# A reciprocal root taken on 128x4 row sums and sent through memory, instead of on a broadcast 128x512 tile

## The chip, the cores and the metric

One core of a Trainium2 chip. The metric is the device time of one execution in microseconds (us); lower is better. Engines in the profile: PE does the matrix products (PEld its weight loads), DVE is the vector engine, ACT the scalar engine, POOL is GpSimd, and SP only issues DMA transfers. A line number such as L277 is a line of the kernel's file; the change shifts the numbers, so the same statement has another number after it.

## The reference

A spectral filter along the sequence, then a gated feed-forward block on the normalized result. Cut to what matters:

```python
X = np.fft.rfft(x, axis=1)              # x: (8, 3008, 256)
y = np.fft.irfft(X * F, n=3008, axis=1) # F: complex filter, (1505, 256)
t = y.reshape(24064, 256)
rms = np.sqrt(np.mean(t * t, axis=-1, keepdims=True) + 1e-06)
xn = t / rms * rms_g
g = xn @ w_gate                         # 256 -> 1536
out = (g * sigmoid(g) * (xn @ w_val)) @ w_out
```

The change is about `1 / rms`: one number for each of the 24064 tokens.

## The kernel before

Both transforms are done as small matrix products with two trips through memory (z and g). Channels lie on the 128 partitions and tokens along the row. A batch has 6 groups (m = 0 to 5) of 512 tokens, the last of 448, and a group has 12 slots of the feed-forward loop, so a batch is 72 slots and the kernel 576. In a slot `gv` makes gate and value, `down` the output product of two slots earlier. Units of the next batch are put into the slots by a table, `plan`, in program order; every engine takes its instructions in that order.

A sum over channels is a sum over partitions. The kernel before takes it with a 128x128 matrix of ones, which leaves the same sum in all 128 partitions, and then raises that full tile to the power -0.5 on POOL:

```python
def q_unit(b, m):
    sq = st[b]["sq"].pop(m)
    w = ntok(m)                                            # 512, or 448 for m == 5
    ps = psM.tile([P, 512], FP32, tag="mx", name="psq")
    for dh in range(2):
        nc.tensor.matmul(ps[:, 0:w], ones, sq[:, dh, 0:w], start=(dh == 0), stop=(dh == 1))
    u = up.tile([P, 512], FP32, tag="u", name="u")
    nc.scalar.activation(out=u[:, 0:w], in_=ps[:, 0:w], func=AXT.Identity, scale=1.0 / D, bias=epsb)
    st[b]["u"][m] = u

def xn_unit(b, m):
    ...
    nc.gpsimd.tensor_tensor(out=rho[:, 0:w], in0=u[:, 0:w], in1=mhalf.to_broadcast([P, w]),
                            op=ALU.pow)                    # L277
    ...
    nc.gpsimd.tensor_tensor(out=xn[:, :, 0:w], in0=y[:, :, 0:w],
                            in1=rho[:, 0:w].unsqueeze(1).to_broadcast([P, 2, w]), op=ALU.mult)  # L280
```

The part of the plan that matters (batch b is prepared while batch b - 1 is multiplied; t = 72 (b - 1)):

```python
for i in range(12):
    at(t + i, a_unit, b, i)                       # first transform; needs x in SBUF
    if i % 3 == 2:
        at(t + i + 1, z_store, b, i // 3)         # SP: 4 stores to memory
for c in range(4):
    at(t + 13 + 2 * c if c < 3 else t + 30, t2_load, b, c)   # SP: loads them back, transposed
for i in range(16):
    s0 = t + 20 + (i * 36) // 16
    at(s0, b_unit, b, i)                          # psb, then two products on DVE
    at(s0 + 3, bi_unit, b, i)                     # psi, evicted by ACT
    ...                                           # g_store at s0 + 5
...                                               # t4_load at t + 60 + c
for m in range(6):
    s0 = t + 64 + 6 * m
    at(s0, n_unit, b, m, 0)                       # psn: y and its squares
    at(s0 + 1, n_unit, b, m, 1)
    at(s0 + 3, q_unit, b, m)
    at(s0 + 4, xn_unit, b, m)
```

Group m of batch b is first used in slot t + 72 + 12 m. Ahead of the slots a prologue prepares batch 0 and its first two groups.

## Time and profile before

| | before |
|---|---|
| median of the runs | 4263.72 us (3 runs, 4261.08 to 4263.81) |
| POOL busy | 4021 of 4261 us, 94% |
| of that, the power | 3851 us, 48 times 71.8 or 81.9 us |
| PE busy | 25% |
| PE's wait for xn | 2010 us |

The page of the kernel before: the busy time of each engine; the rows of POOL and the granted TensorE clock in 40 slices (a digit is tenths); the lines of the chain that ended last.

```profile
PE 1047.3 (25%) x5952; PEld 596.1 (14%) x5952; DVE 589.5 (14%) x903; ACT 628.2 (15%) x1094; POOL 4021.3 (94%) x210
...
POOL 3999989999899998999989999899998999989997
PEclk9995666556655575556655666556655656666566
...
POOL rho L277 90%; POOL xn L280 2%; PE pg L295 1%; PE pv L295 1%; POOL xc L177 0%; DMA xc<-in_x_dram 0%; DMA t_252<-z_tmp 0%; PE psi L220 0%; DMA z_tmp<-t_237 0%; PE psa L185 0%; DMA z_tmp<-t_209 0%; ACT u L269 0%; PE psq L267 0%; PE psb L2
```

POOL is full from the third slice to the end, and the chain that ended last is the power for nine tenths of the span. PE's clock row reads 5 and 6: PE works in bursts and idles between them at half clock.

The groups of instructions by shape (count, then busy us and mean ns, then the idle time ahead of them and what ended it):

```profile
L277 POOL TENSOR_TENSOR rho<-u,mhalf 128x512 f32<-128x512 f32 x40 | 3277.0, 81924 | 186.5 <-ACT u L269 146.8 <-PE po_7988 L312 6.4 <-PE po_9510 L312 6.4
L277 POOL TENSOR_TENSOR rho<-u,mhalf 128x448 f32<-128x448 f32 x8 | 574.1, 71765 | 0.2
...
L280 POOL TENSOR_TENSOR xn<-y,rho 128x1024 f16<-128x1024 f32 x40 | 93.7, 2342 | 3.1
```

Two shapes of the same power give a slope: (81.92 - 71.77) / 64 = 0.159 us per column. A multiplication of twice as many elements on the same engine, L280, takes 2.34 us. So the power is dear per column, and the tile has 128 identical rows. The table of waits (us in total, times, longest) says who pays:

```profile
PE pg L295 <- POOL xn L280: 2010.4, 32, 81.8
```

What would bound the kernel if POOL did not is seen in the bursts. The timeline, plain slots near the end (start, duration; each is the first matmul of a slot):

```profile
4094.94 0.59 PE L295 MATMUL pg<-xn,wg 128*128 128x512 f16 x2
...
4096.24 0.59 PE L295 MATMUL pg<-xn,wg 128*128 128x512 f16 x2
```

A slot takes 1.30 us when PE has nothing to wait for. The table of windows shows the clock over one burst:

```profile
core 0: us, PE busy (x) PEld busy (x) DVE busy (x) ACT busy (x) POOL busy (x), PEclk, DMA share, GB/s
...
2005.00:2010.00 5.00, 5.00 (x19) 2.40 (x18) 2.38 (x4) 1.55 (x3) 4.92 (x2) 0.53 0.86 209
2010.00:2015.00 5.00, 5.00 (x36) 3.31 (x35) 3.34 (x6) 2.63 (x5) 5.00 (x1) 1.00 0.21 53
```

PE is busy for both stretches; in the first its mean granted clock is 0.53, in the second 1.00, and it gets through 36 matmuls instead of 19.

### The profile page before, as it was taken

The numbers are of one execution on the slowest core, as the hardware profiler recorded it, in microseconds if no ns is written. First come the engines' busy times: TensorE is split into PE (matmuls) and PEld (weight loads), VectorE is DVE, ScalarE is ACT, GpSimd is POOL, SyncE is SP. The second block draws the span as 40 slices with busy tenths as digits, with TensorE's granted clock in tenths as the row PEclk, the third lists the DMA queues.
The fourth block names the chain that finished last, engine by engine and source line by source line (L and its number), as shares of the span: only waits on it lengthen the run. The fifth ranks groups of instructions, "written<-read, shape, count | busy, mean of one in ns | idle before, by whom it ended". The sixth has DMA issues, their size and how long they took to land.

```text
span 4261.0 us, 16476 instructions
## 1 busy us (share of the span) xinstructions
PE 1047.3 (25%) x5952; PEld 596.1 (14%) x5952; DVE 589.5 (14%) x903; ACT 628.2 (15%) x1094; POOL 4021.3 (94%) x210
## 2 busy tenths in 40 slices
PE   3031232114221141212312232122311313221023
PEld 1021121002110030101201121011211202111011
DVE  3011110003100130002200121001210102110011
ACT  3021121002110021101111111111101201111011
POOL 3999989999899998999989999899998999989997
PEclk9995666556655575556655666556655656666566
DMA  7020010001100010000100001000110101000000
GB/s 153 0 46 12 16 39 23 12 0 39 29 23 12 10 42 16 23 13 15 38 16 23 13 23 29 16 23 12 25 27 16 36 0 25 25 8 5 0 10 15
DMA packets 82114, 96.78 MB, mean 23 GB/s; under 512 B 9672, under 2 KB 62408, under 8 KB 81744
## 3 DMA queue, kind: packets, MB, share of 16 engines
q1 hardware_dynamic: 71920, 77.95, 7.4%
q0 software_dynamic: 10112, 17.77, 2.5%
q8 instruction: 47, 0.77, 0.1%
q14 instruction: 35, 0.29, 0.0%
HBM read 60.56 MB, written 49.81 MB: 26 GB/s over the span
## 4 chain that ended last, share of the span: by engine, by line
POOL 93%; PE 4%; DMA 1%; issue 1%; ACT 0%; DVE 0%; SPq 0%; POOLq 0%; DVEq 0%; ACTq 0%
POOL rho L277 90%; POOL xn L280 2%; PE pg L295 1%; PE pv L295 1%; POOL xc L177 0%; DMA xc<-in_x_dram 0%; DMA t_252<-z_tmp 0%; PE psi L220 0%; DMA z_tmp<-t_237 0%; PE psa L185 0%; DMA z_tmp<-t_209 0%; ACT u L269 0%; PE psq L267 0%; PE psb L206 0%; PE po_12225 L312 0%
## 5 line engine op out<-in xcount | busy, mean ns | idle before, releaser
L277 POOL TENSOR_TENSOR rho<-u,mhalf 128x512 f32<-128x512 f32 (+1 forms) x48 | 3851.1, 80231 | 186.7 <-ACT u L269 146.8
L295 PE MATMUL pg<-xn,wg 128*128 128x512 f16 (+1 forms) x1152 | 376.8, 412 | 2476.9 <-POOL xn L280 2010.4
L300 DVE TENSOR_TENSOR hh<-pv,sg 128x512 f16<-128x512 f32 (+1 forms) x576 | 390.6, 679 | 3611.9 <-PE pv L295 2217.5
L299 ACT ACTIVATE sg<-pg 128x512 f16<-128x512 f32 (+1 forms) x576 | 339.1, 590 | 2274.7 <-PE pg L295 2272.6
L295 PEld LDWEIGHTS <-wg 128*128 128x128 f16 x1152 | 111.9, 103 | 2512.1 <-issue 2485.7
L295 PE MATMUL pv<-xn,wv 128*128 128x512 f16 (+1 forms) x1152 | 372.2, 407 | 0.0
L312 PEld LDWEIGHTS <-hh 128*128 128x128 f16 (+1 forms) x2304 | 236.7, 104 | 217.3 <-issue 130.6
L269 ACT ACTIVATE u<-psq,epsb 128x512 f32<-128x512 f32 (+1 forms) x48 | 32.6, 678 | 1134.4 <-POOL rho L277 1120.3
L295 PEld LDWEIGHTS <-wv 128*128 128x128 f16 x1152 | 121.6, 106 | 158.4 <-issue 48.0
L280 POOL TENSOR_TENSOR xn<-y,rho 128x1024 f16<-128x1024 f32 (+1 forms) x48 | 110.3, 2297 | 3.8
L206 PEld LDWEIGHTS <-wb 96*128 96x128 f16 x256 | 26.2, 107 | 491.7 <-issue 469.1
L220 PEld LDWEIGHTS <-wi 128*128 128x128 f16 x512 | 52.9, 106 | 112.9 <-issue 71.2
L258 ACT ACTIVATE y<-psn,gsb 128x512 f32<-128x512 f32 (+1 forms) x96 | 65.6, 683 | 19.7 <-PE psn L251 15.2
L185 PE MATMUL psa<-xc,wa 128*128 128x512 f16 x96 | 40.5, 428 | 107.1 <-DMA xc<-in_x_dram 97.8
L260 ACT ACTIVATE sq<-psn 128x512 f16<-128x512 f32 (+1 forms) x96 | 56.5, 589 | 0.0
L177 POOL DMA_DIRECT2D xc<-in_x_dram x64 | 34.8, 558 | 0.8 <-POOLq L474 0.8
L267 PE MATMUL psq<-sq,ones 128*128 128x512 f16 (+1 forms) x96 | 30.2, 394 | 2.3 <-ACT sq L260 2.3
L185 PEld LDWEIGHTS <-wa 128*128 128x128 f16 x96 | 9.8, 103 | 119.1 <-issue 101.0
L312 PE MATMUL po_11699<-wo,hh 128*128 128x256 f16 x24 | 5.3, 307 | 75.1 <-ACT o_11682 L317 75.1
L206 PE MATMUL psb<-t_2390,wb 96*128 96x256 f16 x8 | 2.0, 338 | 72.7 <-ACT u L269 72.7
L206 PE MATMUL psb<-t_3912,wb 96*128 96x256 f16 x8 | 2.0, 337 | 72.7 <-ACT u L269 72.7
L206 PE MATMUL psb<-t_5434,wb 96*128 96x256 f16 x8 | 2.0, 338 | 72.6 <-ACT u L269 72.6
(948 smaller groups left out, 1187.0 us busy)
## 6 DMA issues: line engine op xcount, KB each, us to landing
xc<-in_x_dram POOLq DMA_DIRECT2D x56, 192.0 KB, 4.7
wi<-wi_t SPq DMA_DIRECT2D x4, 512.0 KB, 12.2
xc<-in_x_dram POOLq DMA_DIRECT2D x8, 160.0 KB, 5.4
wb<-wb_t SPq DMA_DIRECT2D x1, 768.0 KB, 5.9
wg<-in_moe_w_gate_dram POOLq DMA_DIRECT2D x4, 192.0 KB, 13.1
wv<-in_moe_w_val_dram POOLq DMA_DIRECT2D x4, 192.0 KB, 12.4
wo<-in_moe_w_out_dram POOLq DMA_DIRECT2D x4, 192.0 KB, 13.2
out_dram<-o_874 SPq DMA_DIRECT2D x2, 256.0 KB, 3.8
```

The lines of the kernel that those rows point to most:

```text
L177: nc.gpsimd.dma_start(t[h * 64:h * 64 + 64, 0:w, :], rows[:, lo:lo + w, :])
L185: nc.tensor.matmul(ps, wa, st[b]["x"][c][:, 2 * r:2 * r + 2, :], start=True, stop=True)
L220: nc.tensor.matmul(ps[:, u, :], wi[:, 2 * i + u, q, :], s12[q][:, u, :], start=(q == 0), stop=(q == 1))
L258: nc.scalar.activation(out=y[:, dh, 0:w], in_=ps[:, 0:w], func=AXT.Identity, scale=gsb[:, dh:dh + 1])
L260: nc.scalar.activation(out=st[b]["sq"][m][:, dh, 0:w], in_=ps[:, 0:w], func=AXT.Square)
L269: nc.scalar.activation(out=u[:, 0:w], in_=ps[:, 0:w], func=AXT.Identity, scale=1.0 / D, bias=epsb)
L277: nc.gpsimd.tensor_tensor(out=rho[:, 0:w], in0=u[:, 0:w], in1=mhalf.to_broadcast([P, w]), op=ALU.pow)
L280: nc.gpsimd.tensor_tensor(out=xn[:, :, 0:w], in0=y[:, :, 0:w], in1=rho[:, 0:w].unsqueeze(1).to_broadcast([P, 2, w]), op=ALU.mult)
L295: nc.tensor.matmul(ps[:, 0:w], wt[:, dt_, ts(jt, P)], xn[:, dt_, 0:w], start=(dt_ == 0), stop=(dt_ == 1))
L299: nc.scalar.activation(out=sg[:, 0:w], in_=pg[:, 0:w], func=AXT.Silu)
L300: nc.vector.tensor_tensor(out=hh[:, 0:w], in0=pv[:, 0:w], in1=sg[:, 0:w], op=ALU.mult)
L312: nc.tensor.matmul(po[s4 // 2][0:w, s4 % 2, :], hh[:, s4 * P:s4 * P + w], wo[:, jt, :], start=(jt == 0 and s4 % 2 == 0), stop=(jt == JT - ...
```

## The change

Its intent: take the power once per token and not 128 times. The squares become the stationary operand and a single column of ones streams, so the sums of 512 tokens come out as a 128x4 tile with tokens on partitions. The power is taken there. To multiply y by it, the 512 numbers are needed along the row of every partition again: the 128x4 tile is stored to memory (16 contiguous bytes per partition) and loaded back with a broadcast to all 128 partitions. The trip takes time, so the plan computes the sums earlier and leaves slots between sums, trip and use. To make room the transform's units move to earlier slots too.

The diff, cut (pools, memory declaration, prologue, the plan of batch 0's later groups and the 448-token case left out):

```diff
     def q_unit(b, m):
         sq = st[b]["sq"].pop(m)
-        for dh in range(2):
-            nc.tensor.matmul(ps[:, 0:w], ones, sq[:, dh, 0:w], start=(dh == 0), stop=(dh == 1))
-        nc.scalar.activation(out=u[:, 0:w], in_=ps[:, 0:w], func=AXT.Identity, scale=1.0 / D, bias=epsb)
+        for q in range(4):
+            for dh in range(2):
+                nc.tensor.matmul(ps[0:w, q:q + 1], sq[:, dh, q * P:q * P + w], ones, ...)
+        nc.vector.tensor_scalar(out=u[0:w, a:e], in0=ps[0:w, a:e], scalar1=1.0 / D,
+                                scalar2=1e-6 * Y_SCALE * Y_SCALE, op0=ALU.mult, op1=ALU.add)
+        nc.gpsimd.tensor_tensor(out=rho, in0=u, in1=mhalf, op=ALU.pow)        # 128x4
+    def rho_move(b, m):
+        nc.sync.dma_start(r_d[b, m], st[b]["u"].pop(m))
+        nc.sync.dma_start(rb.rearrange("p a q -> p (a q)"),
+                          r_d[b, m].rearrange("p q -> (p q)").partition_broadcast(P))
     def xn_unit(b, m):
-        nc.gpsimd.tensor_tensor(out=rho[:, 0:w], in0=u[:, 0:w], in1=mhalf.to_broadcast([P, w]), op=ALU.pow)
-        nc.gpsimd.tensor_tensor(out=xn[:, :, 0:w], in0=y[:, :, 0:w], in1=rho[:, 0:w]..., op=ALU.mult)
+        rv = rb.rearrange("p t q -> p q t")                                   # stride of 16 bytes
+        nc.gpsimd.tensor_tensor(out=xv[:, :, 0:nq], in0=yv[:, :, 0:nq], in1=rv[:, 0:nq]..., op=ALU.mult)
...
+        def norm_plan(b, m, s0):
+            at(s0, n_unit, b, m, 0)
+            at(s0 + 1, n_unit, b, m, 1)
+            at(s0 + 3, q_unit, b, m)
+            at(s0 + 5, rho_move, b, m)
+            at(s0 + 10, xn_unit, b, m)
...
-                at(t + 13 + 2 * c if c < 3 else t + 30, t2_load, b, c)
+                at(t + 13 + c if c < 3 else t + 24, t2_load, b, c)
-                s0 = t + 20 + (i * 36) // 16
+                s0 = t + 16 + 2 * i
-                    at(s0 + 5, g_store, b, i // 2)
+                    at(s0 + 4, g_store, b, i // 2)
-                at(t + 60 + c, t4_load, b, c)
+                at(t + 53, t4_load, b, c)
-                s0 = t + 64 + 6 * m        (n, q and xn units at s0, +1, +3, +4)
+                norm_plan(b, m, t + 57 + 8 * m)
```

More of the change, by code (lines that the diff above doesn't have):

```diff
@@ L129 @@
     g_d = nc.dram_tensor("g_tmp", (B, K2, KR, D), FP16, kind="Internal").ap()
+    r_d = nc.dram_tensor("r_tmp", (B, 6, P, 4), FP32, kind="Internal").ap()
     glob = ctx.enter_context(tc.tile_pool(name="glob", bufs=1))
     xp = ctx.enter_context(tc.tile_pool(name="xp", bufs=4))
-    t1p = ctx.enter_context(tc.tile_pool(name="t1p", bufs=2))
+    t1p = ctx.enter_context(tc.tile_pool(name="t1p", bufs=3))
     t2p = ctx.enter_context(tc.tile_pool(name="t2p", bufs=3))
@@ L139 @@
     sqp = ctx.enter_context(tc.tile_pool(name="sqp", bufs=2))
-    rp = ctx.enter_context(tc.tile_pool(name="rp", bufs=1))
+    rp = ctx.enter_context(tc.tile_pool(name="rp", bufs=2))
     up = ctx.enter_context(tc.tile_pool(name="up", bufs=2))
@@ L159 @@
     gsb = glob.tile([P, 2], FP32)
-    ones = glob.tile([P, P], FP16)
-    mhalf = glob.tile([P, 1], FP32)
-    epsb = glob.tile([P, 1], FP32)
+    ones = glob.tile([P, 1], FP16)
+    mhalf = glob.tile([P, 4], FP32)
     st = {b: {"x": {}, "t1": {}, "t2": {}, "s": {}, "t3": {}, "t4": {}, "y": {}, "sq": {},
@@ L263, in q_unit @@
         sq = st[b]["sq"].pop(m)
-        w = ntok(m)
-        ps = psM.tile([P, 512], FP32, tag="mx", name="psq")
-        for dh in range(2):
-            nc.tensor.matmul(ps[:, 0:w], ones, sq[:, dh, 0:w], start=(dh == 0), stop=(dh == 1))
-        u = up.tile([P, 512], FP32, tag="u", name="u")
-        nc.scalar.activation(out=u[:, 0:w], in_=ps[:, 0:w], func=AXT.Identity, scale=1.0 / D, bias=epsb)
-        st[b]["u"][m] = u
+        ps = psM.tile([P, 4], FP32, tag="mx", name="psq")
+        for q in range(4):
+            w = P if 4 * m + q < H - 1 else 64
+            for dh in range(2):
+                nc.tensor.matmul(ps[0:w, q:q + 1], sq[:, dh, q * P:q * P + w], ones,
+                                 start=(dh == 0), stop=(dh == 1))
@@ new lines, in q_unit @@
+        u = up.tile([P, 4], FP32, tag="u", name="u")
+        rho = up.tile([P, 4], FP32, tag="rho", name="rho")
+        if m == 5:
+            nc.vector.memset(u, 1.0)
+            parts = ((P, 0, 3), (64, 3, 4))
+        else:
+            parts = ((P, 0, 4),)
+        for w, a, e in parts:
+            nc.vector.tensor_scalar(out=u[0:w, a:e], in0=ps[0:w, a:e], scalar1=1.0 / D,
+                                    scalar2=1e-6 * Y_SCALE * Y_SCALE, op0=ALU.mult, op1=ALU.add)
+        nc.gpsimd.tensor_tensor(out=rho, in0=u, in1=mhalf, op=ALU.pow)
@@ L272, in xn_unit @@
+        st[b]["u"][m] = rho
+    def rho_move(b, m):
+        nc.sync.dma_start(r_d[b, m], st[b]["u"].pop(m))
+        rb = rp.tile([P, P, 4], FP32, tag="rb", name="rb")
+        nc.sync.dma_start(rb.rearrange("p a q -> p (a q)"),
+                          r_d[b, m].rearrange("p q -> (p q)").partition_broadcast(P))
+        st[b]["u"][m] = rb
     def xn_unit(b, m):
-        w = ntok(m)
-        u = st[b]["u"].pop(m)
+        rb = st[b]["u"].pop(m)
         y = st[b]["y"].pop(m)
-        rho = rp.tile([P, 512], FP32, tag="rho", name="rho")
@@ L277, in xn_unit @@
-        nc.gpsimd.tensor_tensor(out=rho[:, 0:w], in0=u[:, 0:w], in1=mhalf.to_broadcast([P, w]),
-                                op=ALU.pow)
         xn = xnp.tile([P, 2, 512], FP16, tag="xn", name="xn")
-        nc.gpsimd.tensor_tensor(out=xn[:, :, 0:w], in0=y[:, :, 0:w],
-                                in1=rho[:, 0:w].unsqueeze(1).to_broadcast([P, 2, w]), op=ALU.mult)
+        nq = 4 if m < 5 else 3
+        yv = y.rearrange("p a (q t) -> p a q t", q=4)
+        xv = xn.rearrange("p a (q t) -> p a q t", q=4)
@@ new lines, in xn_unit @@
+        rv = rb.rearrange("p t q -> p q t")
+        nc.gpsimd.tensor_tensor(out=xv[:, :, 0:nq], in0=yv[:, :, 0:nq],
+                                in1=rv[:, 0:nq].unsqueeze(1).to_broadcast([P, 2, nq, P]),
+                                op=ALU.mult)
+        if nq < 4:
+            nc.gpsimd.tensor_tensor(out=xv[:, :, 3, 0:64], in0=yv[:, :, 3, 0:64],
+                                    in1=rv[:, 3, 0:64].unsqueeze(1).to_broadcast([P, 2, 64]),
+                                    op=ALU.mult)
@@ L366 @@
         nc.vector.memset(mhalf, -0.5)
-        nc.vector.memset(epsb, 1e-6 * Y_SCALE * Y_SCALE)
         for c in range(NC):
@@ L405 @@
             q_unit(0, m)
+            rho_move(0, m)
+        for m in range(2):
             xn_unit(0, m)
@@ L414, in at @@
             plan.setdefault(slot, []).append((fn, a))
-        for m in range(2, 6):
-            s0 = (m - 2) * 10
-            at(s0, n_unit, 0, m, 0)
-            at(s0 + 1, n_unit, 0, m, 1)
-            at(s0 + 3, q_unit, 0, m)
-            at(s0 + 4, xn_unit, 0, m)
+        def norm_plan(b, m, s0):
[4 more added lines that the diff above has]
+            at(s0 + 10, xn_unit, b, m)
+        for m in range(2, 6):
+            norm_plan(0, m, (m - 2) * 10)
         for b in range(1, B):
@@ L439 @@
             for c in range(4):
-                at(t + 60 + c, t4_load, b, c)
+                at(t + 53, t4_load, b, c)
             for m in range(6):
-                s0 = t + 64 + 6 * m
-                at(s0, n_unit, b, m, 0)
-                at(s0 + 1, n_unit, b, m, 1)
-                at(s0 + 3, q_unit, b, m)
-                at(s0 + 4, xn_unit, b, m)
+                norm_plan(b, m, t + 57 + 8 * m)
         stores = {}
```

## The prediction

> **What bounds the kernel now.** GpSimd. The page gives POOL 94% busy (4021 of 4261 us), PE 25%; the chain of waits is 90% the power (line 277). The groups by shape give it 81.92 us for 128x512 and 71.77 for 128x448, 48 times, 3851 us. A line through the two sizes is 0.65 us + 0.159 us per column; all 128 rows hold the same numbers (a ones matrix broadcasts the sum). PE waits 2010 us for xn.
>
> **What the change removes, adds, moves.**
> - The power shrinks to 128x4: 0.65 + 4 x 0.159 = 1.3 us (estimate), 62 us in all for 3851.
> - The xn multiplication (2.34 us for 1024 elements) stays on POOL, one operand now at a 16-byte stride. The Trainium skill, "GPSIMD Engine Reference", section 3.1, gives about 2.6 cycles per element for two inputs, near this trace's 2.1 ns; no run shows the stride's cost. I allow 2.3 to 5 us.
> - Row sums become 8 one-column matmuls with 8 weight loads instead of two 512-column ones: 0.45 to 0.85 us (loads of 0.105 us that partly overlap, as in the psn groups), against 0.43. The ACT eviction u (0.68 us) becomes a tiny DVE operation.
> - New: a 2 KB store and a 256 KB broadcast load per tile. Here a 96 KB store lands in 1.9 us, 96 KB loads in 2.2. I estimate 2 + 3 us, with SP blocked 2 us between. Row sums to xn is then about 10 us; a batch's first group has 12 slots (16 us), later ones more. Hidden, except in the prologue.
>
> **Then PE bounds it.** Bursts in the timeline show PE saturated at granted clock 1.00: 1.303 us per slot (gate, value, down), 1.417 in the 448-token groups. Added work: first transform 0.216 us, b and bi 0.65 per pair, psn 0.22.
> Per batch: 60 x 1.303 + 12 x 1.417 = 95; transform 2.6; b and bi 10.4; psn 2.6; row sums 3.9; small stalls 3 (ACT holding the two shared PSUM buffers: slots of 1.97 us instead of 1.74; about 1 us at the first b unit, because z-store to t2 landing takes 7 us and has about 6.5). That is 118. Seven, and a last of 100: 924.
> Prologue: the first power starts at 96.3 us today; power, store, load and xn put the first slot at about 105. Some 3 us for the cold clock (0.5 in the first 4 us of a burst; "TensorE: Matmul & The Clock Gate", part 1, says that sustained activity releases it, and this trace agrees). Tail 6. Sum 1037 us.
>
> **Predicted 1037 us, 1012 to 1085 holding it 8 times in 10.** Faster by over 2%: 0.985, within 2%: 0.01, slower: 0.005.
>
> **What would show it.** Power mean 1 to 2 us; POOL below 30% busy; PE near 95% busy, mean clock above 0.95; chain of waits led by PE lines 295 and 312; first slot at 103 to 108 us; plain slots of 1.30 us; xn not PE's main releaser after the first slot.
>
> **What would make it wrong.** A fixed cost of the small power, or a strided xn, far over these figures, so that xn arrives after its slot; SP blocked by the round trips, so that t2 or t4 loads come late, PE stalls several us a batch and its clock falls; row sums over 1 us a group; a clock that does not hold at 1.00 under steady load.

## The result

The median fell from 4262.4 us (4 runs, 4260.43 to 4263.81) to 1032.17 us (4 runs, 1031.0 to 1034.96). The ratio is 0.2423, with a 95% interval of 0.2417 to 0.2428. Ratios here are the mean time of one kernel's fast runs over that of the other's of the same rounds, so not quite the ratio of the medians quoted. The result is correct.

The page after, the lines that answer to those of before:

```profile
PE 931.7 (90%) x6240; PEld 565.0 (55%) x6240; DVE 591.7 (57%) x966; ACT 597.5 (58%) x1046; POOL 246.0 (24%) x218
...
PE   2162789999999999999999999999999999999997
...
POOL 5501423113410333013410333013410332023200
PEclk9999999999999999999999999999999999999999
...
PE pg L319 21%; PE pv L319 20%; PE psi L221 6%; PE psb L207 3%; ACT sq L261 2%; PE psn L252 1%; PE psa L186 1%; DMA fi_120<-in_filt_i_dram 1%; DMA fi_119<-in_filt_i_dram 1%; PE psq L269 1%; ACT y L259 1%; DVE hh L324 1%; DMA rb<-r_tmp 1%; D
```

POOL went from 94% to 24%. PE is at 9 in every slice from the seventh to the last but one, its clock row is 9 throughout (the run's mean granted clock is 0.997; for its first 117 us see below), and the chain that ended last is led by the gate and value matmuls. The groups:

```profile
L299 POOL TENSOR_TENSOR xn<-y,rb 128x1024 f16<-128x1024 f32 x40 | 114.9, 2873 | 263.5 <-DMA rb<-r_tmp 195.2 <-ACT sg L323 13.2 <-ACT t_8933 L226 10.6
...
L281 POOL TENSOR_TENSOR rho<-u,mhalf 128x4 f32<-128x4 f32 x48 | 48.7, 1015 | 388.1 <-DVE u L279 366.4 <-issue 21.2 <-POOL xn L299 0.3
```

The power takes 1.01 us instead of 81.92: 48.7 us in all for 3851. The xn multiplication, whose one operand is now read at a stride of 16 bytes, takes 2.87 us instead of 2.34. The table of windows, with the columns of the one above, one stretch for the prologue, batch 0, batch 1 and the last batch (the bounds are the starts of the first slots):

```profile
0.00:103.41 103.41, 33.76 (x140) 15.29 (x141) 39.88 (x48) 30.79 (x42) 34.57 (x54) 1.00 0.79 162
103.41:230.78 127.37, 117.64 (x772) 71.14 (x771) 70.05 (x117) 73.51 (x129) 32.14 (x31) 0.99 0.47 106
230.78:346.10 115.32, 113.36 (x782) 69.99 (x781) 71.28 (x120) 73.16 (x130) 27.61 (x22) 1.00 0.46 110
924.59:1031.00 106.41, 100.18 (x649) 58.85 (x648) 54.27 (x88) 54.19 (x95) 18.20 (x10) 0.99 0.19 47
```

In batch 1 PE is busy 113.4 of 115.3 us at a clock of 1.00. Most of PE's idle time in the whole span, 69.7 of 99.3 us, is the prologue. One warning about the clock column: this trace's first record of the clock is at 117.4 us, and the views print 1.00 for all that lies before it. The matmuls say otherwise: those of 512 columns start 0.43 us apart from 112.1 to 116.8 us, and 0.22 us apart from 117.5 us on. So the 1.00 of the prologue says nothing, and the start of batch 0 ran at about half rate. The trip through memory, median time from issue to landing (size, us):

```profile
rb<-r_tmp SPq DMA_DIRECT2D x48, 256.0 KB, 4.0
...
r_tmp<-rho SPq DMA_DIRECT2D x48, 2.0 KB, 2.0
```

And the trip in the timeline for the first group of batch 2: sums (L269), power (L281), store (L285), broadcast load (L287), xn (L299), and the first slot that uses it (L319):

```profile
329.20 0.34 PE L269 MATMUL psq<-ones,sq 128*128 128x1 f16 x8
...
330.37 1.03 POOL L281 TENSOR_TENSOR rho<-u,mhalf 128x4 f32<-128x4 f32 x1 [36.30 <-DVE u L279]
...
331.43 0.34 SPq L285 DMA_DIRECT2D r_tmp<-rho  x1
...
334.02 0.34 SPq L287 DMA_DIRECT2D rb<-r_tmp  x1
...
337.61 2.87 POOL L299 TENSOR_TENSOR xn<-y,rb 128x1024 f16<-128x1024 f32 x1 [6.21 <-DMA rb<-r_tmp]
...
346.10 0.60 PE L319 MATMUL pg<-xn,wg 128*128 128x512 f16 x2
```

From the start of the sums to the end of xn, 340.48, it is 11.3 us, and 5.6 us later the first slot of the batch needs it. PE waits for none of this. What PE does wait for (left out: other waits of the prologue, the longest 22.8 us for its first load of t2, and short waits for DVE and ACT in the slots, some 7 us in all):

```profile
PE psa L186 <- DMA xc<-in_x_dram: 16.6, 2, 10.5
...
PE pg L319 <- POOL xn L299: 6.7, 1, 6.7
...
PE psb L207 <- DMA t_901<-z_tmp: 2.2, 1, 2.2
```

One wait for xn, in the prologue. One of 6.0 us and one of 10.5 us for x (the longer is the start of the kernel). And one wait per batch, seven of 0.9 to 2.2 us (the longest is shown; 10.5 us in all), for the first load of t2. Last, what the new sums cost PE, in plain slots of the last batch:

```profile
941.97 0.59 PE L319 MATMUL pg<-xn,wg 128*128 128x512 f16 x2
...
943.47 0.59 PE L319 MATMUL pg<-xn,wg 128*128 128x512 f16 x2
...
944.77 0.59 PE L319 MATMUL pg<-xn,wg 128*128 128x512 f16 x2
```

The slot with the eight sums takes 943.47 - 941.97 = 1.50 us, the next 1.30: the sums cost 0.20 us, 25 ns for each load with its one-column matmul. The six slots of batch 1 that hold sums are 0.17 to 0.20 us longer than their like, too.

### The profile page after: what moved, and what is told of

It is laid out like the page before. It is cut to its first block, busy times and chain, and to the rows that moved or that the text cites. A ratio compares the mean times of both kernels' runs of the same rounds, so it can differ in the third digit from the quotient of the medians.

```text
span 1031.0 us, 17242 instructions
## 1 busy us (share of the span) xinstructions
PE 931.7 (90%) x6240; PEld 565.0 (55%) x6240; DVE 591.7 (57%) x966; ACT 597.5 (58%) x1046; POOL 246.0 (24%) x218
## 4 chain that ended last, share of the span: by engine, by line
PE 76%; DMA 9%; DVE 5%; ACT 5%; issue 3%; SPq 1%; POOL 0%; ACTq 0%; DVEq 0%; POOLq 0%
PE pg L319 21%; PE pv L319 20%; PE psi L221 6%; PE psb L207 3%; ACT sq L261 2%; PE psn L252 1%; PE psa L186 1%; DMA fi_120<-in_filt_i_dram 1%; DMA fi_119<-in_filt_i_dram 1%; PE psq L269 1%; ACT y L259 1%; DVE hh L324 1%; DMA rb<-r_tmp 1%; DMA fr_114<-in_filt_r_dram 1%; SPq L196 1%
## 5 line engine op out<-in xcount | busy, mean ns | idle before, releaser
L319 PE MATMUL pg<-xn,wg 128*128 128x512 f16 (+1 forms) x1152 | 340.4, 377 | 6.7 <-POOL xn L299 6.7
L319 PE MATMUL pv<-xn,wv 128*128 128x512 f16 (+1 forms) x1152 | 339.4, 376 | 0.0
L336 PEld LDWEIGHTS <-hh 128*128 128x128 f16 (+1 forms) x2304 | 221.9, 98 | 108.9 <-issue 32.7
L299 POOL TENSOR_TENSOR xn<-y,rb 128x1024 f16<-128x1024 f32 (+1 forms) x48 | 132.5, 2760 | 316.6 <-DMA rb<-r_tmp 233.2
L319 PEld LDWEIGHTS <-wv 128*128 128x128 f16 x1152 | 113.2, 98 | 132.3 <-issue 2.5
L281 POOL TENSOR_TENSOR rho<-u,mhalf 128x4 f32<-128x4 f32 x48 | 48.7, 1015 | 388.1 <-DVE u L279 366.4
L319 PEld LDWEIGHTS <-wg 128*128 128x128 f16 x1152 | 105.9, 98 | 29.0 <-issue 7.3
L186 PE MATMUL psa<-xc,wa 128*128 128x512 f16 x96 | 39.0, 412 | 23.6 <-DMA xc<-in_x_dram 16.6
L207 PEld LDWEIGHTS <-wb 96*128 96x128 f16 x256 | 23.7, 101 | 65.4 <-issue 40.6
L186 PEld LDWEIGHTS <-wa 128*128 128x128 f16 x96 | 9.5, 100 | 33.8 <-issue 20.4
L269 PEld LDWEIGHTS <-sq 128*128 128x128 f16 (+1 forms) x384 | 17.4, 97 | 14.4 <-ACT sq L261 4.1
L207 PE MATMUL psb<-t_250,wb 96*128 96x256 f16 x8 | 2.3, 410 | 22.9 <-DMA t_250<-z_tmp 22.8
L269 PE MATMUL psq<-ones,sq 128*128 128x1 f16 (+1 forms) x384 | 17.6, 165 | 3.4 <-ACT sq L261 3.4
L279 DVE TENSOR_SCALAR u<-psq 128x4 f32<-128x4 f32 (+2 forms) x56 | 7.8, 152 | 15.2 <-PE psq L269 14.3
## 6 DMA issues: line engine op xcount, KB each, us to landing
wi<-wi_t SPq DMA_DIRECT2D x4, 512.0 KB, 13.3
wg<-in_moe_w_gate_dram POOLq DMA_DIRECT2D x4, 192.0 KB, 13.3
```

Of the source, the lines that this page charges most:

```text
L186: nc.tensor.matmul(ps, wa, st[b]["x"][c][:, 2 * r:2 * r + 2, :], start=True, stop=True)
L207: nc.tensor.matmul(ps[:, u, :], wb[:, k, :], st[b]["t2"][k // KC][:, k % KC, :], start=True, stop=True)
L269: nc.tensor.matmul(ps[0:w, q:q + 1], sq[:, dh, q * P:q * P + w], ones, start=(dh == 0), stop=(dh == 1))
L281: nc.gpsimd.tensor_tensor(out=rho, in0=u, in1=mhalf, op=ALU.pow)
L299: nc.gpsimd.tensor_tensor(out=xv[:, :, 0:nq], in0=yv[:, :, 0:nq], in1=rv[:, 0:nq].unsqueeze(1).to_broadcast([P, 2, nq, P]), op=ALU.mult)
L319: nc.tensor.matmul(ps[:, 0:w], wt[:, dt_, ts(jt, P)], xn[:, dt_, 0:w], start=(dt_ == 0), stop=(dt_ == 1))
```

## The experiments

My theory: the number of columns of the power was the whole cost; with it gone PE bounds the kernel, and the trip through memory is free because it is issued far enough ahead. Rivals: the new plan, not the power, gave a good part; the trip is partly exposed; the early slots are decoration. Every run below was compared with the kernel before on the same chip, and unless said otherwise the times are medians of 4 fast runs. All results were correct.

**plan_only: the plan without the small power.** The kernel before with the new slots for t2, b, bi, g, t4 and the norm units; the first-transform pool stays at 2 buffers, because, by the author's account, a third does not fit beside the wide tiles (no run on record shows it).

```diff
-                s0 = t + 64 + 6 * m
+                s0 = t + 57 + 8 * m      # xn at s0 + 10; power still 128x512; b and t4 slots as in the change
```

> The kernel before with the change's slot plan alone; the power stays 128x512. Mine (the width of the power is the cause): POOL still runs 48 powers of about 80 us back to back, so 4245 to 4285 us, POOL above 92% busy. Rival (the new plan gives a good part of the gain): clearly below 4000 us.

Measured: 4155.16 us, a single run of unknown state, against 4262.19. I missed: by this one run, the plan alone is worth 107 us, 2.5%. POOL's busy time is the same, 4021.4 us. What fell is its idle time, as its table of waits shows:

```profile
POOL rho L277 <- ACT u L269: 78.3, 9, 46.4
```

46.4 of these 78.3 us are in the prologue. In the kernel before the same wait was 146.8 us, with 38 us of similar waits put down to PE beside it. In the old plan the sums of a batch's first group stand in slot 67, seven slots into the last group of the batch before; POOL had finished all it had by then. In the new plan they stand in slot 60. (That this is the reason is read from the slots and the waits; no run tests it alone.) So the plan helped even a POOL-bound kernel, but the rival's size (below 4000 us) is refuted: the power's width is the cause of the rest.

**old_slots: the small power in the old slots.**

```diff
-            at(s0 + 5, rho_move, b, m)
-            at(s0 + 10, xn_unit, b, m)
+            at(s0 + 3, rho_move, b, m)
+            at(s0 + 4, xn_unit, b, m)
...
-                norm_plan(b, m, t + 57 + 8 * m)
+                norm_plan(b, m, t + 64 + 6 * m)     # t2, b, bi, g and t4 slots as before, too
```

> The small power and the round trip, but every slot number of the kernel before: norm units at 64 + 6m, store, load and xn straight after the row sums. In the profile after, row sums to the end of xn take 11.2 us; here a batch's first group has about 7 us from row sums to use. Mine: PE waits about 4 us for xn once per batch, its clock halves for some us, while the waits of PE for t2 (10.5 us in all) go away: 1045 to 1080 us. Rival (the early slots are decoration, the wait for t2 is all they cost): 1018 to 1031 us.

Measured: 1067.43 us (1062.02 to 1072.06), ratio 0.2504 [0.2495, 0.2512]: 35 us slower than the change. PE's table of waits:

```profile
PE pg L319 <- POOL xn L299: 33.3, 8, 6.8
```

6.8 us of that is the prologue, as in the change; the other 26.5 us are seven waits of 3.5 to 4.3 us, one at the head of each later batch. My theory held in size. One part of it did not hold: the waits for t2 were to go away, and six of 0.5 to 1.5 us remain (5.6 us in all, against 10.5). The run also gives the split of the gain: of 3230 us, 3195 come from the small power and its trip in the old slots (with the change's buffers and prologue), 35 from the new slots.

**pow_plus24 and pow_plus80: a delay that did not delay.** I wanted to lengthen the trip of each batch's first group by a known time, with an idle power of 24 or 80 columns ahead of the real one:

```diff
+        if m == 0:
+            nc.gpsimd.tensor_tensor(out=rb...[:, 0:80], in0=gsb[:, 0:1].to_broadcast([P, 80]),
+                                    in1=mhalf[:, 0:1].to_broadcast([P, 80]), op=ALU.pow)
         nc.gpsimd.tensor_tensor(out=rho, in0=u, in1=mhalf, op=ALU.pow)
```

> The change, with an idle 128x24 power ahead of the real one in the first group of each batch, so that xn comes later there. By the line through 4 and 512 columns it takes 4.2 us, less than the 5.6 us that xn of a batch's first group ends before its use. Mine: only the prologue pays, 1033 to 1040 us, and no wait of PE for xn in later batches. Rival (the trip is partly exposed already, so any delay shows): 7 times 4 us more, 1060 us or more.

> The same with 128x80: 13.1 us by the line, 7.5 us more than the slack. Mine: PE waits 7 to 8 us for xn in each of the seven later batches, 13 us more in the prologue, and about 2 us of cold clock each time: 1095 to 1130 us. Rival (slack is larger than I read, or the power has a different cost per column): below 1080 us, or a power far from 13 us.

Measured: 1030.81 us (1030.09 to 1033.92) and 1032.98 us (1031.86 to 1033.99), as fast as the change. The second missed my expectation, and the timeline of pow_plus80 shows that the experiment was at fault:

```profile
58.81 13.13 POOL L284 TENSOR_TENSOR rb<-gsb,mhalf 128x80 f32<-128x80 f32 x1 [1.00 <-DMA gsb<-in_moe_rms_g_dram]
...
94.80 1.01 POOL L287 TENSOR_TENSOR rho<-u,mhalf 128x4 f32<-128x4 f32 x1 [22.85 <-DVE u L279]
```

The added power reads only constants, so POOL started it as soon as it was free. It was done at 71.94 us, and POOL then sat idle for 22.85 us until the row sums were there; in the later batches it was done 19 to 27 us ahead. It stood in no chain. The runs did give the cost of the power at two more widths, 4.18 and 13.13 us; the line through 4 and 512 columns (1.01 and 81.92 us) gives 4.2 and 13.1.

**pow_chain24 and pow_chain80: the same delay, in the chain.** The added power now reads the row sums:

```diff
-                                    in0=gsb[:, 0:1].to_broadcast([P, 80]),
+                                    in0=u[:, 0:1].to_broadcast([P, 80]),
```

> The earlier dummy power read only constants, so POOL ran it in idle time ahead of the row sums and nothing was delayed. Here it reads the row sums, so it stands in the chain of a batch's first group. 128x24 took 4.18 us, less than the 5.6 us of slack read from the profile after. Mine: only the prologue pays, 1034 to 1041 us, no wait of PE for xn in later batches. Rival (the trip is already partly exposed): 1060 us or more.

> The same with 128x80, 13.13 us. Mine: 7.5 us beyond the slack, so seven waits of PE for xn of 7 to 8 us, about 2 us of cold clock with each, 13 us in the prologue: 1095 to 1130 us. Rival (the slack is larger than read): below 1080 us.

Measured: 1038.44 us (1034.94 to 1040.07), ratio 0.2435 [0.2430, 0.2440], and 1112.35 us (1109.98 to 1114.11), ratio 0.2611 [0.2607, 0.2615]. In pow_chain24 PE waits for xn once, in the prologue (10.7 us instead of 6.7); in pow_chain80 eight times (the first line below is of pow_chain24, the second of pow_chain80):

```profile
PE pg L327 <- POOL xn L307: 10.7, 1, 10.7
...
PE pg L327 <- POOL xn L307: 69.8, 8, 20.1
```

Of the eight, one wait of 20.1 us is the prologue; the other seven are 6.7 to 7.7 us. So a delay of 4.2 us in each batch is free, one of 13.1 us costs about 7, and the slack is about 6 us, as read from the trace. The 80 us lost are 63 us of added waits (69.8 - 6.7) and some 17 us more, about 2 us for each wait; the first slot after a wait takes 2.8 to 3.2 us here, where the change has 1.5 to 1.7. The granted clock is 0.50 in such a stretch (249.28 to 252.00 us of this trace), as at the start of the bursts of the kernel before.

**no_lead: without the slots between sums, trip and xn.**

```diff
-            at(s0 + 5, rho_move, b, m)
-            at(s0 + 10, xn_unit, b, m)
+            at(s0 + 3, rho_move, b, m)
+            at(s0 + 3, xn_unit, b, m)
```

> The change, but store, load and xn are issued in the slot of the row sums instead of 2 and 7 slots after; the row sums keep their early slots. Mine (what hides the trip is how early the row sums are, the spacing behind them only changes which in-order queue waits): 1026 to 1040 us. Rival (the spacing keeps SP and POOL from blocking the transfers of the transform, so PE stalls): 1045 us or more, with PE waiting for t2 or t4 loads.

Measured: 1085.32 us (1085.09 to 1086.11), ratio 0.2547 [0.2543, 0.2552], 53 us slower than the change. Here the rival won:

```profile
PE psb L207 <- DMA t<-z_tmp: 75.1, 8, 23.8
```

23.8 us of it is the prologue. In each of the seven later batches PE waits 7.0 to 8.0 us for the first t2 load, 51.3 us in all against 10.5 in the change. These 41 us more are most of the 53; the rest is not itemized, but the mean granted clock is 0.974 here against 0.997. The timeline of the change, at the row sums of the fourth group (m = 3, L269), with the last stores of z (L196), the load of t2 (L200) and its first use (L207):

```profile
483.45 2.79 SPq L196 DMA_DIRECT2D z_tmp<-t_5546  x4
483.52 0.34 PE L269 MATMUL psq<-ones,sq 128*128 128x1 f16 x8
...
487.86 0.32 SPq L200 DMA_DIRECT2D t_5638<-z_tmp  x1
...
491.19 0.38 PE L207 MATMUL psb<-t_5638,wb 96*128 96x256 f16 x2 [1.88 <-DMA t_5638<-z_tmp]
```

The same stretch in no_lead, with the store (L285) and load (L287) of the trip:

```profile
506.41 0.34 PE L269 MATMUL psq<-ones,sq 128*128 128x1 f16 x8
...
508.71 0.34 SPq L285 DMA_DIRECT2D r_tmp<-rho  x1
...
511.16 0.34 SPq L287 DMA_DIRECT2D rb<-r_tmp  x1
...
511.59 1.78 SPq L196 DMA_DIRECT2D z_tmp<-t  x4
...
519.72 0.59 PE L207 MATMUL psb<-t,wb 96*128 96x256 f16 x2 [7.52 <-DMA t<-z_tmp]
```

In the change the last z stores are issued as the sums begin. In no_lead the trip's two transfers stand ahead of them in SP's queue. SP takes its queue in order: it waits for the power, then for the store to land, and only then issues the z stores, 5.2 us after the sums began. The b matmuls come 13.3 us after the sums instead of 7.7. The Trainium skill, "DMA: Bandwidth & Descriptors" (anatomy of one DMA), says that a semaphore wait is made on the issuing sequencer ahead of dispatch and not by the DMA engines; this run shows what that costs when something else is queued behind.

**no_lead_but3: the spacing given back to the fourth group alone.**

```diff
+            late = m == 3
-            at(s0 + 3, rho_move, b, m)
-            at(s0 + 3, xn_unit, b, m)
+            at(s0 + 5 if late else s0 + 3, rho_move, b, m)
+            at(s0 + 10 if late else s0 + 3, xn_unit, b, m)
```

> Without the spacing cost 1085 us. If that is only because the store and load of a batch's fourth group (m = 3) stand ahead of the last z stores in SP's in-order queue (5 us later there by the trace), then giving that one group its spacing back, and no other, brings 1026 to 1038 us. Rival (the blocking is general, of SP by all groups or of POOL): 1045 us or more.

Measured: 1033.18 us (1030.45 to 1037.7), ratio 0.2425 [0.2418, 0.2432]: the change's time. The 53 us came from this one place of the queue; the other five groups do without the spacing. (The run gives that group's xn on POOL its spacing back too; that SP's order is what matters is read from the timelines above.)

**x_early: the loads of x for batch 1 issued earlier.** The 6.0 us wait for x in batch 0's first slot: the loads stood on POOL behind the second xn, which waits for its trip.

```diff
+        for c in range(NXC):
+            x_load(1, c)
         for c in range(NXC):
             t4_load(0, c)
...
-        for c in range(NXC):
-            x_load(1, c)          # was behind the two xn units of the prologue
```

> The change, with the loads of x for the second batch issued ahead of the first power instead of behind the second xn on the in-order POOL queue. Mine: the 6.0 us wait of PE for xc in the first slot goes, and the clock warms up earlier: 1022 to 1027 us. Rival (that wait hides another one): 1029 to 1033 us.

Measured: 1026.08 us (1025.29 to 1027.97), ratio 0.2408 [0.2404, 0.2411]: 6 us faster than the change. Only the wait at the start of the kernel is left of the two (the change had 16.6 us in two):

```profile
PE psa L186 <- DMA xc<-in_x_dram: 10.9, 1, 10.9
```

**b_later: the b units one slot later,** to do away with the seven waits for t2.

```diff
-                s0 = t + 16 + 2 * i
+                s0 = t + 17 + 2 * i
```

> The change, with the b, bi and g-store units one slot later. Mine: the seven waits of PE for the first t2 load (0.9 to 2.2 us, 10.5 in all) go: 1019 to 1026 us. Rival (the delay comes back at the t4 loads and the psn matmuls, four slots after the last g store): 1030 us or more.

Measured: 1035.03 us (1033.25 to 1037.31), ratio 0.2430 [0.2426, 0.2434], the same as the change. I missed. PE's waits:

```profile
PE psb L207 <- DMA t<-z_tmp: 24.8, 4, 22.8
...
PE psi L221 <- DVE s L213: 15.7, 24, 2.0
...
PE po L336 <- DVE o L343: 4.8, 8, 0.6
```

22.8 us of the first line is the prologue, so the t2 waits did fall, from 10.5 us to 2.0. They came back elsewhere, but not where the rival said (psn's waits for t4 grew by 0.9 us in all). The wait of psi for DVE is 11.0 us in the run "best" below and 15.7 here, and eight waits of the output product for DVE's eviction are new. One slot moves the b units from even slots to odd ones, and DVE evicts the output in an odd slot of each group.

**best: both loads of time taken out.** x_early, and the b units two slots later, which keeps them even.

```diff
-                s0 = t + 16 + 2 * i
+                s0 = t + 18 + 2 * i       # and the x loads as in x_early
```

> x loads early, and b, bi and g-store units two slots later, which keeps them on the same even and odd slots (one slot later put the b units into the slots where DVE evicts the output). Mine: 6 us less as in the x run, and the seven t2 waits (10.5 us) gone: 1013 to 1020 us. Rival (the two slots come back as waits for t4 at psn, or in DVE and ACT): 1024 us or more.

Measured: 1014.5 us (1012.88 to 1015.98), ratio 0.2380 [0.2377, 0.2384]: against the change's 0.2423 it is 1.8% faster, and it beats both kernels. Of the waits for t2 and for x only those of the prologue are left:

```profile
PE psb L207 <- DMA t<-z_tmp: 23.8, 1, 23.8
...
PE psa L186 <- DMA xc<-in_x_dram: 10.7, 1, 10.7
```

A power on DVE for the wide tile, which would need no trip, was built as well; the compiler did not take it, so that stays open; the record has no trace of this attempt.

## Why the prediction was right

The forecast was 1037 us; 1032 was measured, inside the range. Step by step:

| step | predicted | measured |
|---|---|---|
| power on 128x4 | 1.3 us | 1.01 us |
| xn with the strided operand | 2.3 to 5 us | 2.87 us |
| row sums on PE, a group | 0.45 to 0.85 us | 0.20 us |
| store and load of the trip | 2 + 3 us | 2.0 + 4.0 us |
| sums to xn | about 10 us, hidden | 11.3 us, hidden with 5.6 us to spare |
| plain slot | 1.30 us at clock 1.00 | 1.30 us, mean clock 0.997 |
| first slot | 105 us | 103.4 us |
| batch 0 | 118 + 3 us | 127.4 us |
| batches 1 to 6, each | 118 us | 115.1 to 116.1 us |
| last batch with the tail | 106 us | 106.4 us |

- **What bounded it, and what would next.** Right. The power went from 3851 to 48.7 us, old_slots shows that the small power gives 3195 us before any slot is moved, and PE bounds the steady batches: busy 98% of batch 1.
- **The trip is hidden.** Right, and tested: 4.2 us more in the chain costs nothing in a steady batch, 13.1 us costs about 7.
- **Stalls.** The 1 us at the first b unit was right in place and near in size (0.9 to 2.2 us). What I had not seen is that batch 0's first slot waits 6.0 us for x, and the slots behind it run cold (2.56 and 2.85 us): batch 0 took 127.4 us where I had 121. In x_early, where the wait is gone, batch 0 takes 117.6 us.
- **The term that was mis-sized the other way: the row sums.** "0.45 to 0.85 us (loads of 0.105 us that partly overlap...)" took the length of one weight load for its rate. Eight loads with eight one-column matmuls lengthen a slot by 0.20 us. The Trainium skill, "TensorE: Matmul & The Clock Gate" (part 1), says that start to start never falls below about 25 ns however few columns; the trace agrees: the eight matmuls start 25 ns apart, 0.20 us for eight, and so do their loads, each listed at 96 ns. Some 0.45 us less in each of six groups is 2.7 us a batch, about what a steady batch stayed under my 118. So there are two errors of opposite sign, +6 us in batch 0 and -14 us over the six steady batches, beside a prologue 1.6 us shorter; the sum was better than its terms. (The rounded terms add up to 1040, not to the 1037 that I wrote.)
- **"PE near 95% busy"** was wrong: 90%. My own sum has a prologue of a tenth of the span with PE busy for a third of it (33.8 of 103.4 us).
- **"SP blocked by the round trips, so that t2 or t4 loads come late"** was listed as what would break the forecast. In the change it does not happen, and no_lead shows that it is what the spacing of one group prevents: 53 us.

## What to carry to other kernels

When an operation is dear per column, look whether its input repeats along the partitions: taking it once per value, on a tile with the values spread over partitions, can be worth a trip through memory of several us if the result is needed later than that. Then read two things from the trace: the slack between the end of the new chain and its first use, and what stands behind each of its transfers in the same in-order queue, because a transfer that waits holds up everything behind it. After a large step the next few per cent lie in the positions of single units, and moving one by an odd number of slots can give back as much as it gains.

## What the Trainium skill lacked or had wrong

- "GPSIMD Engine Reference" gives cycles per element for simple element-wise operations, none for a power. The power costs 0.159 us per column of a 128-row tile (1.01 us at 4 columns, 4.18 at 24, 13.13 at 80, 71.77 at 448, 81.92 at 512), where a two-input multiplication costs 2.34 us for 1024. Section 3.1's figure of about 2.6 cycles per element, at 1.2 GHz an estimate of 2.2 ns, is near that multiplication's 2.3 ns.
- The same page, section 7, on kernels for POOL's own cores, puts a read of SBUF with a step of over 8 bytes at about 2.9 cycles per element instead of 1.9, 50% more; the prediction did not use this row. It has no case with one strided operand of two: here, with one at a stride of 16 bytes (and one dimension more), the multiplication of 1024 elements took 2.87 us instead of 2.34, 23% more. No run separates the stride from the dimension.
- "TensorE: Matmul & The Clock Gate", on LDWEIGHTS, makes a load of 128 columns an estimate of 107 ns (columns over 1.2). In these traces the costliest groups of loads have means of 97 to 107 ns, but a load and a one-column matmul together cost 25 ns in a row of eight. The page's floor of about 25 ns was the figure to use; the load's time is not its rate.
- By the same formula a load of 64 columns takes half as long, an estimate of 53 ns; these traces list it at 106 ns. The groups of 448 tokens, which have one such load in each slot, take 1.42 us per slot against 1.30 us for 512 tokens, with 0.2 us of idle ahead of that load in the trace of before. That the load is the cause is not shown.
- "DMA: Bandwidth & Descriptors" has a fixed cost of about 2 us, fitted to transfers that POOL issues; the 2 KB store, issued by SP, takes the same (2.0 us). No page puts a price on a store and a dependent load in a queue that others use: 53 us here, in no_lead.
